# The opening loads of a fused attention and feed-forward kernel: weights in two pieces, the first pair in halves, V by pairs, and one later load

## The chip, the cores and the metric

The kernel runs on one core of one Trainium2 chip. The metric is the device time of one execution in microseconds (us), as a median over several executions. A core has five engines that run their own instruction streams and wait for each other through semaphores: TensorE (PE, matrix products), VectorE (DVE), ScalarE (ACT, activation functions), GpSimd (POOL) and SyncE (SP, which here only issues DMAs). [...]

## The reference

The reference computes cosine attention and then a feed-forward layer with the activation h * cos(h). B = 8 batches, H = 12 heads, S = 448 positions, D = 64; the model width is 768, the hidden width 2048.

```python
q_n = q / (norm(q) + 1e-6);  k_n = k / (norm(k) + 1e-6)      # over D
scores = q_n @ k_n.T / tau
attn = softmax(scores)
x = (attn @ v) as [B*S, H*D]                                  # 3584 x 768
h = x @ w_in                                                  # 768 x 2048
out = (h * cos(h)) @ w_out                                    # 2048 x 768
```

## The kernel before

**Units and pairs.** The 12 heads of a batch are two units of six heads, so there are 16 units, u0 to u15. A unit is three pairs of heads; the 48 pairs are numbered g = 0 to 47, and pair g works on two heads at once. Six pairs make one batch. In the text below "the third pair of unit 3" is g = 11, the twelfth pair of all.

**Normalisation of a pair.** `load` (L596) fetches k into partitions 0 to 63 and q into partitions 64 to 127 of a float32 buffer `raw`; there are two such buffers, so unit u + 2 can be loaded for a pair only after unit u has been scaled for it. Each partition holds seven blocks of 64 numbers for each head. `square` (L629) squares into `sq`, on ACT for the first pairs and on POOL later. `reduce` (L643) sums on DVE. `rnorm` (L654) makes the reciprocal root, with two activations on ACT (L667, L670: logarithm and exponential) or with an addition and a power on POOL (L663, L664), by the list `roots`. `scale` (L673) multiplies into the bfloat16 buffer `qks`, on POOL; for the very first pair POOL takes the first four blocks (half a) and DVE the last three (half b). `transposes` (L691) turns the pair: for g below 9 PE transposes into PSUM (bank TP, a part of the tile MP) and DVE copies to `qkT` (L716); from g = 9 on a DMA transpose that SP issues does it (L695).

**Attention of a pair.** `scores` (L719) makes four score tiles on PE (L735 a half one, L727 three full ones), and ACT takes their exponentials into `PX` (L742). `attend` (L801) multiplies with V on PE (L821, L828, and the row sums at L845 and L858); ACT makes the reciprocal of the sums (L887 and L889, or L901 and L903) and DVE or POOL writes the normalised, transposed x into `xT` (L893, L907, L940).

**Feed-forward.** `m1` (L960) is the first product, x @ w_in, for one batch: 16 blocks of 128 hidden columns in eight steps of two, each of six accumulated matmuls (L953). The n-th block needs the weight quarter n // 4. After each step ACT takes the cosine (L982) and DVE the product (L984) into `gT`; the key ("gT", 0, y) stands for step y of batch 0. The second product (L1052 and L1081) is cut into small pieces, which fill PE's time between the scores of the later pairs. Its weights W2 come in four quarters, its result leaves through `osb` (L1019, L1016) and SP.

**Loads.** All q and k loads are issued by SP, in a fixed order. V (`load_v`, L609) and the weights (`load_w1`, L1098, and `load_w2`, L1104) are issued by POOL. V of one unit is two DMAs of 192 KB; W1 comes in four quarters of 768 KB, W2 in four. The first pair's k and q are two loads on SP (`apart`), each with its own semaphore; V of unit 0 waits until the first q has landed, V of unit 1 and the first two quarters of W1 until half a of the first pair has been scaled (key ("qks", 0, 0, 0)).

**Order.** A planner (`Program.arrange`, L152) plays the program with costs for each instruction and DMA, and each engine's stream is then emitted in the order of that play. So a change of a load, a gate or a cost can move instructions on every engine. PE additionally gets filler matmuls (L1111) where the play leaves it idle before the first product. The order of the rest, the six pairs of batch 0, then the first product of batch 0, then pairs 6 to 47 with the second product between them, and a first product after every sixth pair or so, is written out at the end of the program (L1242 to L1324).

## Time and profile before

| | |
|---|---|
| median of 3 executions | 416.63 us (415.61 to 416.63) |
| profiled execution | 415.4 us, span 413.6 us |
| granted PE clock | 1.00 in every stretch |
| PE busy | 404.6 us (98%) |
| POOL busy | 248.5 us (60%) |
| ACT busy | 270.2 us (65%) |
| bytes moved by DMA | 63.99 MB, mean 155 GB/s |

The profile is of one execution. The time of that execution is 1.8 us more than its span, which runs from the first to the last instruction. "Busy" is the sum of an engine's instructions. PE's sum counts pipelined matmuls, so it says that PE had something to do, not that it ran at its peak. In rows of instructions in order of time the first number is the start in us from the span's start, the second the time taken, and in brackets stands how long the engine idled before it and what released it. In rows of DMA issues the last number is the time from issue to landing.

### The profile page before, as it was taken

What the parts mean: (1) busy time and instruction counts of PE and PEld (TensorE: products, weight loads), DVE (VectorE), ACT (ScalarE), POOL (GpSimd) and SP (SyncE); (2) the same over time, 40 slices, a digit from 0 to 9 for tenths busy, and PEclk for the clock granted to TensorE, in tenths of its full rate; (3) what the DMA queues carried; (4) which work ended last, traced back from release to release, by engine and by line L of the source; (5) the groups of instructions that cost most, each with busy time, mean ns of one, the idle gap of its engine ahead of it and who ended that gap; (6) DMA issues with size and microseconds to landing.
All of it is one profiled execution on the core that took longest, in us unless ns stands there. A gap on an engine that the chain in (4) does not pass through costs nothing.

```text
span 413.6 us, 13910 instructions
## 1 busy us (share of the span) xinstructions
PE 404.6 (98%) x6213; PEld 243.8 (59%) x6213; DVE 199.9 (48%) x279; ACT 270.2 (65%) x384; POOL 248.5 (60%) x196
## 2 busy tenths in 40 slices
PE   7899999999999999999999999999999999999997
PEld 3354556655566655765567656865567655655555
DVE  4574653426664457445644567344742344413421
ACT  5897578985889745985497647884488745623500
POOL 4999995894776985988489656946482303020000
PEclk9999999999999999999999999999999999999999
DMA  8999999489997999586988975797933531151023
GB/s 183 248 252 226 207 222 202 136 157 215 178 163 164 228 258 188 121 205 149 206 101 188 268 132 113 135 215 188 169 51 79 147 85 32 46 139 38 2 73 81
DMA packets 78736, 63.99 MB, mean 155 GB/s; under 512 B 41844, under 2 KB 72404, under 8 KB 78676
## 3 DMA queue, kind: packets, MB, share of 16 engines
q1 hardware_dynamic: 60468, 50.42, 54.4%
q0 software_dynamic: 18048, 12.59, 20.7%
q8 instruction: 49, 0.80, 0.8%
q10 hardware_dynamic: 160, 0.10, 0.1%
q14 instruction: 11, 0.09, 0.1%
HBM read 55.44 MB, written 11.19 MB: 161 GB/s over the span
## 4 chain that ended last, share of the span: by engine, by line
PE 91%; POOL 3%; ACT 2%; DVE 2%; DMA 1%; issue 0%; SPq 0%; ACTq 0%; POOLq 0%
PE MP L1052 27%; PE SC L953 20%; PE AV L953 12%; PE SC L727 7%; PE AV L764 5%; PE MP L1081 4%; PE AV L788 4%; PE SC L1081 3%; PE MP L953 2%; PE AV L837 2%; POOL qks L678 1%; PE SC L735 1%; ACT cosb L982 1%; PE MP L852 1%; PE AV L1081 1%; DMA raw<-in_q_dram 1%
## 5 line engine op out<-in xcount | busy, mean ns | idle before, releaser
L742 ACT ACTIVATE PX<-SC 128x448 bf16<-128x448 f32 (+1 forms) x192 | 148.7, 825 | 16.0 <-PE SC L727 10.9
L1052 PE MATMUL MP<-W,gT 64*64 64x384 bf16 x2816 | 136.2, 323 | 0.7 <-DVE qkT L716 0.6
L1052 PEld LDWEIGHTS MP<-W,gT 64*64 64x64 bf16 x2816 | 80.1, 107 | 34.5 <-issue 3.9
L953 PE MATMUL SC<-xT,W 128*128 128x448 bf16 x444 | 90.9, 353 | 0.0
L678 POOL TENSOR_TENSOR qks<-raw,rn 128x896 bf16<-128x896 f32 (+1 forms) x48 | 79.8, 1679 | 12.0 <-ACT rn L670 11.6
L640 POOL TENSOR_TENSOR sq<-raw 128x896 bf16<-128x896 f32 x44 | 73.9, 1686 | 11.8 <-DMA raw<-in_q_dram 6.4
L940 POOL TENSOR_TENSOR xT<-xu,RB 128x448 bf16<-128x448 f32 x36 | 40.1, 1135 | 67.7 <-DMA RB<-scr 67.7
L953 PEld LDWEIGHTS SC<-xT,W 128*128 128x128 bf16 x444 | 43.1, 98 | 40.2 <-ACT osb L1016 0.4
L982 ACT ACTIVATE cosb<-SC,cst 128x896 f32<-128x896 f32 x37 | 37.2, 1006 | 37.8 <-PE SC L953 35.9
L953 PE MATMUL AV<-xT,W 128*128 128x448 bf16 x276 | 59.6, 352 | 0.0
L647 DVE TENSOR_REDUCE n<-sq 128x14 f32<-128x896 bf16 (+2 forms) x49 | 51.6, 1059 | 7.1 <-ACT sq L638 4.8
L984 DVE TENSOR_TENSOR gT<-SC,cosb 128x896 bf16<-128x896 f32 x37 | 40.3, 1090 | 28.2 <-ACT cosb L982 28.1
L727 PE MATMUL SC<-qkT 64*64 64x448 bf16 x576 | 51.9, 354 | 0.3
L982 ACT ACTIVATE cosb<-AV,cst 128x896 f32<-128x896 f32 x23 | 23.1, 1006 | 37.1 <-PE AV L953 35.4
L774 DVE COPY xu<-AV 128x448 f32<-128x448 f32 x36 | 22.5, 624 | 50.4 <-PE AV L756 50.4
L953 PEld LDWEIGHTS AV<-xT,W 128*128 128x128 bf16 x276 | 26.6, 98 | 25.4 <-DVE xs L799 1.1
L764 PE MATMUL AV<-PX,va 64*64 64x448 bf16 x432 | 38.2, 349 | 0.0
L614 POOL DMA_DIRECT2D va<-in_v_dram x32 | 22.0, 694 | 22.9 <-DVE gT L984 18.2
L1019 DVE COPY osb<-MP 128x384 f32<-128x384 f32 x26 | 14.5, 558 | 43.9 <-PE MP L1052 32.8
L984 DVE TENSOR_TENSOR gT<-AV,cosb 128x896 bf16<-128x896 f32 x23 | 25.0, 1087 | 20.3 <-ACT cosb L982 20.3
L727 PEld LDWEIGHTS SC<-qkT 64*64 64x64 bf16 x576 | 16.7, 106 | 13.0 <-ACT PX L742 6.3
L775 DVE TENSOR_TENSOR xu<-xu,AV 128x448 f32<-128x448 f32 x36 | 22.4, 621 | 1.2
(84 smaller groups left out, 364.7 us busy)
## 6 DMA issues: line engine op xcount, KB each, us to landing
raw<-in_k_dram SPq DMA_DIRECT2D x48, 224.0 KB, 5.4
raw<-in_q_dram SPq DMA_DIRECT2D x48, 224.0 KB, 5.9
out_dram<-osb SPq DMA_DIRECT2D x54, 192.0 KB, 3.1
RB<-scr SPq DMA_DIRECT2D x22, 336.0 KB, 5.2
va<-in_v_dram POOLq DMA_DIRECT2D x32, 192.0 KB, 6.1
W<-in_moe_w_in_dram POOLq DMA_DIRECT2D x4, 768.0 KB, 15.0
W<-in_moe_w_out_dram POOLq DMA_DIRECT2D x4, 768.0 KB, 20.0
qkT<-qks SPq DMA_TRANSPOSE x39, 4.4
```

The lines of the kernel that those rows point to most:

```text
L640: pool(lambda e, x=x, y=y: e.tensor_tensor(y, x, x, ALU.mult), src_, dst, 0.1 + n * 1.78e-3, label="sq%d.%d" % (u, p)).pad = LATE if u > 1 ...
L647: dve(lambda e, w=w: e.tensor_reduce(out=n2v[i][:, 2 * p : 2 * p + 2, w], in_=sqv[p][:, :, w, :], axis=mybir.AxisListType.X, op=ALU.add), ...
L678: f = lambda e, s0=s0, s1=s1: e.tensor_tensor(qksv[i][:, p, s0:s1].rearrange("p s h d -> p h s d"), rawv[i][:, h, s0:s1, :], bass.AP(rn[i] ...
L727: m = e.matmul(SCv[z][BP * o : BP * o + BP, a, 0:S], t[r, c - 1 + (NT3 + 1) * o, 0:BP], t[r, :, BP : 2 * BP], start=True, stop=True)
L742: act(lambda e: e.activation(PHv[j] if c == 0 else PXv[j][:, c - 1], SCv[z][:, :, 0:n], ACT.Exp, scale=1.0 / TAU), ["SC%d" % z], [("PX", j ...
L764: m = e.matmul(AVv[64 * a : 64 * a + 64, o, 0:S], vav[y][r, 2 * p + a, c + 1, :], PXv[j][r, c, a, :], start=(c == 0), stop=False)
L940: f = lambda e, p=p: e.tensor_tensor(xTv[b % 2][:, UP * i + p, :].rearrange("p (s o m) -> p o s m", s=NB, o=2), xuv[:, u % 3, p, :].rearra ...
L953: t = e.matmul(ph[:, a, 0:S], W1v[:, order[c], 128 * n : 128 * n + 128], xTv[b % 2][:, order[c], :], start=(c == 0), stop=(c == NKC - 1))
L982: act(lambda e, ph=ph, cz=cz: e.activation(cosv[cz], ph[:, :, 0:S], ACT.Sin, bias=cst.ap()[:, 0:1], scale=1.0), names(gi) + ["cst0"], [("c ...
L984: dve(lambda e, ph=ph, cz=cz, gi=gi: e.tensor_tensor(gTv[:, 2 * gi : 2 * gi + 2, S * (b % 2) : S * (b % 2) + S], ph[:, :, 0:S], cosv[cz], ...
L1052: r = e.matmul(POH[b][x : x + 64, 0:HW], gTv[k, y, col + x : col + x + 64], W2v[k, y, HW * b : HW * b + HW], start=(y == 0 and h == 0), st ...
L1081: r = e.matmul(po[:, 0 : w[1] - w[0]], gTv[:, y, col : col + 128], W2v[:, y, w[0] : w[1]], start=(y == 0), stop=(y == NF - 1))
```

## The change

1. *Weights.* `load_w1` takes the cuts from a list, `w1`: two loads of 1024 columns (1.5 MB each) instead of four of 512. The first product's blocks 0 to 7 wait for the first, blocks 8 to 15 for the second. POOL issues the first after the scale of the fourth pair (the first of unit 1), the second after the scale of the fifth; before, the first quarter was issued ahead of the second pair's scale.
2. *First pair.* k and q of the first pair come in halves, four blocks and three; SP issues k's halves and ACT q's halves. ACT does so before it loads its activation table. The square of each half waits only for its own half, and is followed by that half's norm; ACT's squares of the second and third pair come after both.
3. *V.* V of unit 0 comes as two DMAs for its first pair, issued when k's first half has landed, and two for the other two pairs, issued after half a of the first pair is scaled, ahead of V of unit 1.
4. *Unit 3's third pair.* Its k and q load waits for step 5 of the first product of batch 0 (its sixth block pair), its square, sum and scale follow later on POOL and DVE, and its norm goes to ACT. Unit 4's first load waits for step 7 instead of step 6.
5. *Planner.* Some of its constants and rules are changed (issue times, how two queues share, when POOL's first DMAs start), which moves instructions. On PE the fillers are 32 instead of 38; in the first six pairs the first matmuls of a pair's product with V (L821) stand before the next pair's scores instead of behind them in some places; from pair 6 to 8 the pieces of the second product stand in other places between the scores. On DVE the second pair's reduction stands behind the first pair's half b scale and first copy, the third pair's behind its second copy; one reduction (unit 3's third pair) no longer stands before the third copy at the end of the first product. From the second first product on (batch 1) PE's order is the same.

```diff
-    "u4": (6,),
+    "u4": (7,),
...
+    "gates": "xcccac",
+    "openers": ("SP", "ACT"),
+    "v0": ((0, 1), (1, 3)),
+    "together": 1,
+    "w1": (0, 2, 4),
+    "split3": {2: 5},
...
-    "roots": (3, (8, 0), (10, 0), (12, 0), (14, 0)),
+    "roots": ((3, 0), (3, 1), (8, 0), (10, 0), (12, 0), (14, 0)),
...
-    TAKEOFF = {"SP": 1.85, "ACT": 1.85, "POOL": 1.6}
+    TAKEOFF = {"SP": 1.85, "ACT": 1.85, "POOL": 1.9}
...
+        if apart:
+            for z in range(2):
+                s0, s1 = blocks((z,))
+                for x, t in enumerate((k, q)):
+                    go = lambda e, x=x, t=t, s0=s0, s1=s1: e.dma_start(
+                        rawv[i][BP * x : BP * x + BP, h, s0:s1, :].rearrange("p h s d -> p h (s d)"),
+                        bass.AP(t.tensor, ((u // 2) * NH + UH * (u % 2) + 2 * p0) * S * D + s0 * D, [[NB * D, BP], [S * D, 2], [1, (s1 - s0) * D]]))
+                    dma(PLAN["openers"][x], [go], list(reads), [("part", x, z)] + (["first"] if x == 0 and z == 0 else []), "part%d_%d" % (x, z),
...
+        if u == 0:
+            for (p0, p1), reads in zip(PLAN["v0"], reads):
+                dma("POOL", [lambda e, z=z, p0=p0, p1=p1: e.dma_start(
...
+                    list(reads), [("vp", p) for p in range(p0, p1)], "vp%d" % p0, 0.707 * (p1 - p0), "load v u0", None)
+            return
...
     def load_w1(x, behind=None, reads=()):
-        w = FF // NQ
+        c0, c1 = [FF // NQ * y for y in PLAN["w1"][x : x + 2]]
         dma("POOL", [lambda e: e.dma_start(
-            W1v[:, :, w * x : w * x + w], bass.AP(moe_w_in.tensor, w * x, [[FF, 128], [128 * FF, NKC], [1, w]]))],
...
+            W1v[:, :, c0:c1], bass.AP(moe_w_in.tensor, c0, [[FF, 128], [128 * FF, NKC], [1, c1 - c0]]))],
...
-    loads(3)
+    for x in range(UP):
+        if x not in PLAN["split3"]:
+            load(3, x, x + 1)
     norms(3, 0)
...
+    for x, y in PLAN["split3"].items():
+        load(3, x, x + 1, reads=[("gT", 0, y)])
+        square(3, x, "P")
+        reduce(3, x)
     norms(3, 1)
```

## The prediction

> **What bounds the kernel now.** I read the page's first two parts, then busy time by stretch, then each engine's instructions in order of time up to the first product, then the DMA issues.

> ```profile
> span 413.6 us, 13910 instructions
> PE 404.6 (98%) x6213; PEld 243.8 (59%) x6213; DVE 199.9 (48%) x279; ACT 270.2 (65%) x384; POOL 248.5 (60%) x196
> ```
> ```profile
> 10.00:20.00 10.00, 8.03 (x105) 3.72 (x104) 5.49 (x8) 8.49 (x18) 10.00 (x8) 1.00 1.22 247
> 20.00:30.00 10.00, 9.82 (x161) 5.73 (x163) 6.81 (x10) 9.46 (x19) 9.96 (x8) 1.00 1.18 253
> 30.00:40.00 10.00, 9.99 (x114) 4.61 (x113) 4.89 (x8) 8.76 (x15) 9.97 (x10) 1.00 1.22 229
> 50.00:60.00 10.00, 9.21 (x128) 5.65 (x130) 5.77 (x7) 6.66 (x8) 9.75 (x9) 1.00 1.16 219
> 300.00:350.00 50.00, 49.99 (x881) 30.90 (x883) 20.39 (x27) 34.05 (x46) 18.24 (x14) 1.00 0.36 81
> ```
> Columns: stretch, its length, busy PE, PEld, DVE, ACT, POOL, then granted clock, DMA share, GB/s. PE has no room in the late stretches (49.99 of 50), and the changed kernel gives it the same work there. So only the head can move: from 10 to 40 POOL is full, ACT nearly, and the DMA engines are saturated, while PE has small work and fillers; from 50 to 60 PE loses 0.79 us. What the head gains, the end gains, unless a later stall eats it.

> ```profile
> 5.44 1.04 ACT L638 ACTIVATE sq<-raw 128x512 bf16<-128x512 f32 x2 [3.44 <-DMA raw<-in_q_dram]
> 9.25 0.95 ACT L638 ACTIVATE sq<-raw 128x896 bf16<-128x896 f32 x1 [0.55 <-DMA raw<-in_q_dram]
> 11.35 0.31 ACT L667 ACTIVATE rn<-n,cst 128x14 f32<-128x14 f32 x1 [0.71 <-DVE n L647]
> 11.98 1.35 ACT L742 ACTIVATE PX<-SC 128x448 bf16<-128x448 f32 x2
> 13.77 2.16 ACT L742 ACTIVATE PX<-SC 128x896 bf16<-128x896 f32 x3 [0.43 <-PE SC L727]
> 34.70 1.70 ACT L742 ACTIVATE PX<-SC 128x896 bf16<-128x896 f32 x2
> ```
> ```profile
> 7.52 1.04 POOL L678 TENSOR_TENSOR qks<-raw,rn 128x512 bf16<-128x512 f32 x1 [0.34 <-ACT rn L670]
> 8.86 1.35 POOL L614 DMA_DIRECT2D va<-in_v_dram  x2 [0.30 <-POOL qks L678]
> 10.17 0.89 POOL L1100 DMA_DIRECT2D W<-in_moe_w_in_dram  x1
> 11.05 1.73 POOL L678 TENSOR_TENSOR qks<-raw,rn 128x896 bf16<-128x896 f32 x1
> 20.89 0.90 POOL L1100 DMA_DIRECT2D W<-in_moe_w_in_dram  x1
> 25.98 1.70 POOL L678 TENSOR_TENSOR qks<-raw,rn 128x896 bf16<-128x896 f32 x1
> ```
> Each row is start, duration, instruction. ACT idles 3.44 us for the first q, 0.71 and 0.43 us more around the first exponentials, and has no gap over 0.21 us from there to the last pair's. POOL's last scale of the six pairs ends at 27.7, but that pair's exponentials run only up to 36.4: from the second pair on the head is ACT's, and POOL runs ahead of it.

> **The change part by part.**

> *First pair in halves on two queues.*
> ```profile
> raw<-in_k_dram SPq DMA_DIRECT2D x1, 224.0 KB, 3.6
> raw<-in_q_dram SPq DMA_DIRECT2D x1, 224.0 KB, 3.8
> ```
> k is issued at 0.72 and lands at 4.3; q, issued at 1.54, lands at 5.35, so 224 KB take about 1.0 us. The first halves hold 4 of 7 blocks, 256 KB of 448: q's last 192 KB (0.86 us) need not be waited for. Landing 4.5; bounds 3.9 (k's half and q's half moving side by side at k's rate) and 5.35 (no gain). The second halves still land near 5.35. ACT now issues two loads (0.6 to 0.76 us each) ahead of its table load (1.28 us): done by 3.5, hidden before 4.5.

> The norm of half a then ends some 0.8 us earlier: ACT takes half b's square first, at 5.35, so 5.9 instead of 6.5. The scale of half a starts at 6.7, not 7.52.

> *The order on DVE and ACT.*
> ```profile
> 8.30 1.09 DVE L647 TENSOR_REDUCE n<-sq 128x14 f32<-128x896 bf16 x1 [1.05 <-ACT sq L638]
> 10.23 1.09 DVE L647 TENSOR_REDUCE n<-sq 128x14 f32<-128x896 bf16 x1
> 11.24 0.35 DVE L716 COPY qkT<-AV 128x384 bf16<-128x384 bf16 x1
> 11.64 0.29 PE L735 MATMUL SC<-qkT 64*64 64x224 bf16 x4 [0.26 <-DVE qkT L716]
> ```
> Before, two reductions for later pairs stand ahead of the first pair's second copy; after, one does. Scale a 6.7 to 7.75, transposes to 8.2, copy to 8.65, reduction to 9.7, copy to 10.05: first scores at 10.1, not 11.64. But ACT now squares the third pair (its q lands at 9.25, ends 10.2) before the second pair's norm, so exponentials start at 10.7. The first pair's four then end at 10.7 + 3 x 0.87 + 0.45 + 0.5 (the third pair's norm between them) = 14.3; before, at 13.77 + 2 x 0.87 = 15.5. Lead 1.2 us; I take 1.1, as the second pair's scores come only just in time (scale 10.7 to 12.4, transposes 13.1, copy 13.8).

> *POOL.* V of unit 0 is four issues instead of two (1.35/2 = 0.68 each, +1.35), W1 two instead of four (-1.8). After scale a at 7.75 stand four V issues, 8.0 to 10.7; W1's issue at 10.17 is gone. The second pair's scale starts at 10.7, not 11.05: POOL gains only 0.35 us. Up to the last scale (25.98) it has the same work, so that ends at 27.35, against exponentials due at about 31: hidden. The split V hides too: its first pair, issued at 4.4, is wanted at 13, and DMAs of 192 KB issued at 5.65 landed from 12.6.

> *W1 in two.* The first product needs its first load.
> ```profile
> 34.06 1.69 PE L953 MATMUL MP<-xT,W 128*128 128x448 bf16 x8
> W<-in_moe_w_in_dram POOLq DMA_DIRECT2D x1, 768.0 KB, 20.9
> W<-in_moe_w_in_dram POOLq DMA_DIRECT2D x1, 768.0 KB, 15.2
> va<-in_v_dram POOLq DMA_DIRECT2D x1, 192.0 KB, 14.5
> q0 software_dynamic: 890, 0.90, 75.8%
> q1 hardware_dynamic: 548, 0.87, 41.2%
> ```
> (The last two rows: packets and MB of POOL's and SP's queue from 24 to 31.) Before, quarter one lands at 31.1, quarter two at 20.89 + 15.2 = 36.1. Now both are one load, issued near 18.9. As V of unit 1 keeps POOL's queue busy until 9.5 + 14.5 = 24.0, nothing is lost by the later issue: the queue carries the same bytes, and would finish at 36.1. Out of the way are unit 3's third q and k, 0.46 MB at 250 GB/s: 34.2, the late bound. The rows give the other: 890 packets of POOL's queue went beside 548 of SP's, and the new packets hold twice the bytes; with this ratio kept POOL's queue moves 1.25 MB in those 7 us instead of 0.90, and 1.57 MB take 8.8 us, from 23.7 to 32.5, the early bound. PE comes to it at 34.06 - 1.1 = 32.95. I take 32.5, since only the packet rows show both queues at once: no stall. At 34.2 it would cost 1.2 us, all of the lead.

> [...]

> *Unit 3's third q and k behind block six; its norm from POOL to ACT.*
> ```profile
> 27.71 0.59 SPq L599 DMA_DIRECT2D raw<-in_k_dram  x1
> 55.09 1.08 DVE L647 TENSOR_REDUCE n<-sq 128x14 f32<-128x896 bf16 x1
> 56.08 0.61 DVE L716 COPY qkT<-MP 128x896 bf16<-128x896 bf16 x1
> 56.84 1.50 PE L1052 MATMUL MP<-W,gT 64*64 64x384 bf16 x32 [0.64 <-DVE qkT L716]
> 57.20 2.62 POOL L664 TENSOR_TENSOR rn<-rn,cst 128x14 f32<-128x14 f32 x1
> 68.35 1.25 SPq L695 DMA_TRANSPOSE qkT<-qks  x1
> 78.44 0.27 PE L735 MATMUL SC<-qkT 64*64 64x224 bf16 x4
> ```
> The reduction at 55.09 leaves its place before the copy that the second product waits for: copy at 55.8, 0.25 us won. The two issues (27.71, 1.6 us) move to about 51; behind them SP has only unit 4's first load, itself put one block later, and a transpose at 59.5 held by PE. Landing 59, square, unit 4's square (its load lands about 65), scale to 68, transpose at 68.4 as before, landed by 73, wanted at 78.44: 5 us of cover. POOL loses 2.9 us of power; ACT gets 0.5 us of norm near 63, beside a full PE: nothing, at most 0.5.

> *Second product's first tile.* Its pieces stand earlier between the scores after 57, so W2's last quarter is wanted near 61.5 instead of 63.5.
> ```profile
> 42.00 0.80 POOL L1106 DMA_DIRECT2D W<-in_moe_w_out_dram  x1
> W<-in_moe_w_out_dram POOLq DMA_DIRECT2D x1, 768.0 KB, 20.5
> ```
> It landed at 62.5; 1.85 us come off it for the moved q and k, and go on again when these land at 59: between 60.6 and 62.5, so nothing to 1 us. I take nothing, since POOL now issues all of W2 some 5 us earlier. Six of PE's 38 fillers go; they stood in idle time.

> *Sum.* -1.1 (head) -0.25 (copy) = -1.35 us. The profiled execution took 415.4 (span 413.6): 414.05. It ran 1.2 under the median of 416.63; put against the median it gives 415.3. I forecast 415.2.

> **Rivals.**
> 1. *The weights take the head's place.* W1's first load lands at 34.2 by bytes alone, PE waits for it, and only the copy's 0.25 to 0.6 remain: 416.2. For it: the DMA share of 1.2 all through the head. Against: the packet rows.
> 2. *Slower: a descriptor costs the same whatever its size.* Then the four half loads take 4.0 us instead of 2.0, the third pair lands at 11.2, the exponentials start at 12.7, 0.7 later than now, and W1 is 2 us later too: the first product starts between 34.75 and 36.2 (W1's late bound), which less the copy's 0.25 gives 417.1 to 418.5, 417.8 in the middle. It decides once the third pair lands after 10.5. Against: a queue at 1.8 KB and one at 1 KB packets share the engines at 250 GB/s, so time goes with bytes.
> 3. *More than forecast.* The halves move side by side (3.9), unit 2's loads no longer share with W1, and PE's other waits from 56 to 64 close: 0.8 more, 414.4 or under.

> [...]

> **How the numbers follow.** Forecast 45%, rival 1 25%, rival 3 15%, rival 2 10%, and 5% for W1 after 35. A measurement tells about 0.3%, 1.25 us, from no change, so 415.4 is the edge to faster: four fifths of the forecast and all of rival 3 lie beyond it, 0.52; the rest of the forecast and rival 1 make 0.33; 0.15 slower. Range 413.3 (rival 3 from the profiled time) to 417.3, short of rival 2; the forecast's own 414.1 to 416.

> **What would show it.** Right: ACT's first square near 4.5, exponentials from 10.7, the first L953-type product at 33.0 with no wait on a W load, the second product's first row near 55.5. Wrong: an idle row of PE released by W's DMA before the first product, the third pair's square after 10, or a wait on qkT at the twelfth pair's scores.

## The result, and the profile after

| | median of 22 | lowest and highest | profiled execution |
|---|---|---|---|
| kernel before | 416.07 us | 415.32 to 417.34 | 415.4 us, span 413.6 |
| changed kernel | 417.96 us | 415.28 to 420.59 | 416.0 us, span 414.2 |

The changed kernel takes 1.0047 of the time of the kernel before (95% interval 1.0032 to 1.0063): it is slower by 1.9 us, where 1.35 us less had been forecast, and 417.96 lies above the forecast's range (413.3 to 417.3). The second thing to see is the scatter: 5.3 us between the lowest and the highest run, against 2.0 before. The profiled execution is a lucky one, near the lowest of all. Two more profiles were therefore taken, of executions of 415.4 and 419.58 us; the last is slower than 18 of the 22 runs and shows what a slow one loses. In two of the kernels below, one run lay over 1.5% above the fastest of its kernel (422.18 and 421.99 us) and is left out of their ratios.

The changed kernel's page, and its busy time by stretch (columns as in the prediction):

```profile
span 414.2 us, 13901 instructions
PE 405.2 (98%) x6207; PEld 243.6 (59%) x6207; DVE 200.3 (48%) x279; ACT 269.5 (65%) x386; POOL 245.0 (59%) x194
```
```profile
30.00:40.00 10.00, 7.80 (x95) 3.38 (x95) 3.62 (x6) 6.64 (x12) 9.98 (x10) 1.00 1.12 220
50.00:60.00 10.00, 9.44 (x116) 5.59 (x118) 6.32 (x8) 6.06 (x7) 6.33 (x6) 1.00 1.19 226
60.00:70.00 10.00, 10.00 (x252) 6.57 (x247) 4.80 (x7) 8.99 (x15) 3.36 (x2) 1.00 1.14 202
200.00:250.00 50.00, 49.48 (x828) 30.34 (x826) 26.55 (x35) 32.96 (x45) 36.22 (x28) 1.00 0.86 170
```
From 50 to 70 PE gained 0.5 us (9.21 and 9.72 before). From 30 to 40 it lost 2.2, and 0.4 from 200 to 250. The head in order of time, ACT first, then POOL, then PE:

```profile
4.14 0.63 ACT L670 ACTIVATE sq<-raw 128x512 bf16<-128x512 f32 x1 [0.69 <-DMA raw<-in_k_dram]
5.67 0.52 ACT L670 ACTIVATE sq<-raw 128x384 bf16<-128x384 f32 x1 [0.90 <-DMA raw<-in_k_dram]
9.65 0.95 ACT L670 ACTIVATE sq<-raw 128x896 bf16<-128x896 f32 x1 [1.07 <-DMA raw<-in_q_dram]
10.51 0.29 ACT L701 ACTIVATE rn<-n,cst 128x14 f32<-128x14 f32 x1
10.95 1.33 ACT L777 ACTIVATE PX<-SC 128x896 bf16<-128x896 f32 x2
33.18 1.71 ACT L777 ACTIVATE PX<-SC 128x896 bf16<-128x896 f32 x2
```
```profile
6.78 1.04 POOL L712 TENSOR_TENSOR qks<-raw,rn 128x512 bf16<-128x512 f32 x1 [0.94 <-ACT rn L704]
11.19 1.69 POOL L712 TENSOR_TENSOR qks<-raw,rn 128x896 bf16<-128x896 f32 x1 [0.45 <-ACT rn L704]
19.39 0.89 POOL L1135 DMA_DIRECT2D W<-in_moe_w_in_dram  x1
```
```profile
10.13 0.29 PE L770 MATMUL SC<-qkT 64*64 64x224 bf16 x4 [0.35 <-DVE qkT L751]
34.81 1.69 PE L988 MATMUL MP<-xT,W 128*128 128x448 bf16 x8 [2.20 <-DMA W<-in_moe_w_in_dram]
```
The last pair's exponentials stand at 33.18 instead of 34.70: the head has its gain, 1.5 us. Then PE waits 2.20 us for W1's first load, and the first product starts at 34.81 instead of 34.06. And the second scale, which the forecast had at 10.7, stands at 11.19 and waits for ACT: there the second pair's roots (10.51) stand behind the third pair's square, and that waited 1.07 us for its load.

The execution of 419.58 us, what PE waited for after the first product's place, and the rows:

```profile
PE AV L988 <- DVE gT L1019: 1.7, 1, 1.7
PE MP L988 <- DMA W<-in_moe_w_in_dram: 1.5, 1, 1.5
PE MP L1087 <- issue: 0.7, 1, 0.7
PE MP L1087 <- DVE qkT L751: 0.4, 1, 0.4
```
```profile
19.20 0.28 PE L856 MATMUL AV<-PX,va 64*64 64x224 bf16 x1 [0.78 <-DMA va<-in_v_dram]
35.22 1.69 PE L988 MATMUL MP<-xT,W 128*128 128x448 bf16 x8 [1.49 <-DMA W<-in_moe_w_in_dram]
73.80 0.67 PE L1087 MATMUL MP<-W,gT 64*64 64x384 bf16 x10 [0.71 <-issue]
293.51 2.43 PE L988 MATMUL AV<-xT,W 128*128 128x448 bf16 x12 [1.75 <-DVE gT L1019]
```
Four stops of different kinds: V of unit 0's second and third pair late (issued at 8.20, its second DMA landed at 19.15), W1 late, 0.71 us of "issue" (PE waits for no engine and no load that the profile shows), and at 293.51 a product that waits for DVE behind a chain of q and k loads which SP issued late (one at 285.04 that stands at 280.65 in the execution of 416.0 us). The kernel before has none of them.

W1's landing can be read from the DMA rows. From 24 to 31 us, the window of the prediction's two packet rows, POOL's queue moved this in the execution of 416.0 us:

```profile
q0 software_dynamic: 524, 1.07, 80.9%
q1 hardware_dynamic: 385, 0.63, 28.7%
```
That is 1.07 MB where the forecast's early bound had 1.25, and 1.4 packets to one of SP's instead of 1.6. V of unit 1, which stands ahead of W1 in this queue, landed at 24.56 us; 1.57 MB more at 1.07 MB in 7 us take 10.3 us, which gives 34.8, and W1 landed at 34.76.

So it pays to cut every profile in two: the start of the first product, and the rest of the span.

| profiled execution | first product starts | rest of the span |
|---|---|---|
| kernel before | 34.06 | 379.5 |
| changed, 416.0 us | 34.81 | 379.4 |
| changed, 415.4 us | 33.57 | 380.0 |
| changed, 419.58 us | 35.22 | 382.6 |

### The profile page after: what moved, and what is told of

The parts are those of the page before. It is cut to its first block, busy times and chain, and to the rows that moved or that the text cites. A ratio compares the mean times of both kernels' runs of the same rounds, so it can differ in the third digit from the quotient of the medians.

```text
span 414.2 us, 13901 instructions
## 1 busy us (share of the span) xinstructions
PE 405.2 (98%) x6207; PEld 243.6 (59%) x6207; DVE 200.3 (48%) x279; ACT 269.5 (65%) x386; POOL 245.0 (59%) x194
## 3 DMA queue, kind: packets, MB, share of 16 engines
HBM read 55.44 MB, written 11.19 MB: 161 GB/s over the span
## 4 chain that ended last, share of the span: by engine, by line
PE 88%; DMA 5%; POOL 2%; ACT 2%; DVE 1%; SPq 1%; issue 0%; ACTq 0%; POOLq 0%
PE MP L1087 27%; PE SC L988 20%; PE AV L988 12%; PE SC L762 6%; PE AV L799 5%; PE MP L1116 4%; PE AV L823 4%; DMA W<-in_moe_w_in_dram 4%; PE SC L1116 3%; PE MP L988 2%; PE AV L872 2%; DMA raw<-in_q_dram 1%; POOL qks L712 1%; PE SC L770 1%; ACT cosb L1017 1%; PE AV L1116 1%
## 5 line engine op out<-in xcount | busy, mean ns | idle before, releaser
L777 ACT ACTIVATE PX<-SC 128x448 bf16<-128x448 f32 (+1 forms) x192 | 148.8, 825 | 15.9 <-PE SC L762 10.3
L1087 PEld LDWEIGHTS MP<-W,gT 64*64 64x64 bf16 x2816 | 80.2, 107 | 33.8 <-issue 3.7
L674 POOL TENSOR_TENSOR sq<-raw 128x896 bf16<-128x896 f32 x44 | 73.8, 1687 | 16.1 <-DMA raw<-in_q_dram 10.9
L1017 ACT ACTIVATE cosb<-SC,cst 128x896 f32<-128x896 f32 x37 | 37.2, 1006 | 38.1 <-PE SC L988 36.2
L1054 DVE COPY osb<-MP 128x384 f32<-128x384 f32 x26 | 14.5, 558 | 43.1 <-PE MP L1087 31.9
L645 POOL DMA_DIRECT2D va<-in_v_dram x30 | 20.6, 691 | 18.1 <-DVE gT L1019 18.1
## 6 DMA issues: line engine op xcount, KB each, us to landing
raw<-in_k_dram SPq DMA_DIRECT2D x47, 224.0 KB, 4.8
raw<-in_q_dram SPq DMA_DIRECT2D x47, 224.0 KB, 5.1
out_dram<-osb SPq DMA_DIRECT2D x54, 192.0 KB, 3.4
va<-in_v_dram POOLq DMA_DIRECT2D x30, 192.0 KB, 6.8
W<-in_moe_w_out_dram POOLq DMA_DIRECT2D x4, 768.0 KB, 19.7
```

The source lines that it names most:

```text
L674: pool(lambda e, x=x, y=y: e.tensor_tensor(y, x, x, ALU.mult), src_, dst, 0.1 + n * 1.78e-3, label="sq%d.%d" % (u, p)).pad = LATE if u > 1 ...
L777: act(lambda e: e.activation(PHv[j] if c == 0 else PXv[j][:, c - 1], SCv[z][:, :, 0:n], ACT.Exp, scale=1.0 / TAU), ["SC%d" % z], [("PX", j ...
L1017: act(lambda e, ph=ph, cz=cz: e.activation(cosv[cz], ph[:, :, 0:S], ACT.Sin, bias=cst.ap()[:, 0:1], scale=1.0), names(gi) + ["cst0"], [("c ...
L1087: r = e.matmul(POH[b][x : x + 64, 0:HW], gTv[k, y, col + x : col + x + 64], W2v[k, y, HW * b : HW * b + HW], start=(y == 0 and h == 0), st ...
```

## The experiments

"Order held" means that the planner's order on every engine was kept and only the named instructions were exchanged, split or joined; otherwise the planner made a new order. A ratio below is not the quotient of the two medians given with it, so the two can differ a little. Five theories came up in turn: A, W1's first load is late and all the loss is there; B, the moved third load; C, the halves and V hold up the third pair; D, TensorE's own instructions come late; E, no part, but the newly planned order that goes with them.

### Second and third profile of the changed kernel

> The changed kernel once more, unaltered, for a second profiled execution. Theory A (the weights): W1's first 1.5 MB load lands after TensorE wants it; it landed at 34.8 us in the profile of a 416.0 us execution, and the scatter of the runs (415.3 to 420.6) is the scatter of this landing. So in an execution of about 418 us TensorE stands some 4 us ahead of the first product (2.2 in the one seen), the load lands at 36 to 37 us, and what follows the first product is as before to 0.3 us. Theory B (the moved third q and k load of unit 3 and the second product's new order): the stop ahead of the first product is again about 2.2 us, and a slower execution has its loss behind 50 us.

> The changed kernel again, for a third profiled execution; the first two had only 416.0 and 415.4 us, among runs of which half are over 417.9. Theory A (W1's first load lands late): if this one is slow, TensorE's stop ahead of the first product is 3 us or more (2.2 and 1.5 in the two seen). Theory C (the third pair's landing): ScalarE's square of the third pair starts at 10.2 us or later (9.65 and 9.14 in the two seen), GpSimd's second scale at 11.8 us or later, and the last exponentials start over 33.8 us. Theory D (TensorE's own instructions come late): gaps on TensorE behind 50 us that no engine and no load ends, 1 us and more together.

Measured: 417.88 us (415.4 to 420.3, 12 runs), ratio 1.0052 (1.0032 to 1.0073); profiled at 415.4 and, in the other run, at 419.58. The slow one has a stop for W1 of only 1.49 us, ACT's third square at 9.80 and the second scale at 11.34: neither A nor C explains the 4 us between the two. Part of it (0.71) is D, and 1.75 us is a fourth cause.

### W1 in quarters, or in three loads, in the changed kernel

```diff
-W1.0: quarters 0, 1 | W1.1: quarters 2, 3              # changed kernel
+q0, q1 in the place of W1.0 | q2, q3 in that of W1.1   # quarters
+q0 in the place of W1.0 | q1 in that of W1.1 | q2+q3 ahead of W2's first   # three loads
```

> The changed kernel with every engine's order held, but each of W1's two loads issued as two loads of 768 KB, one right behind the other, and the first product's steps waiting for their own quarter. Theory A: the first quarter lands at 30 to 32 us, TensorE's stop ahead of the first product falls from 2.2 us to under 0.5, the median to 413.6 to 415.0 us, and the runs lie as close together as those of the kernel before (within some 2 us). Theory B: no gain, 417 us or more.

> The changed kernel with its order held, W1 in three loads: the first quarter where the first load was, the second quarter where the second load was, the other half behind GpSimd's next square, so that GpSimd issues no more loads ahead of its last scale than in the changed kernel. Theory A: the first quarter lands at 30 to 31.5 us, TensorE's stop ahead of the first product falls below 0.5 us, median 415.0 to 416.0 us (1.9 to 2.9 below the changed kernel). Theory C: at most 0.5 us of that, 417.4 us or more. Theory D: no gain, 417.5 us or more, with gaps behind 50 us.

Measured: quarters 418.38 us, ratio 1.0058 (1.0037 to 1.0080); three loads 420.11, ratio 1.0080 (1.0056 to 1.0105). Both took the stop for W1 away, and neither won anything. PE of the kernel with three loads, and the TensorE clock (the number after the five busy times) around its second gap:

```profile
33.26 1.69 PE L988 MATMUL MP<-xT,W 128*128 128x448 bf16 x8
67.39 0.35 PE L872 MATMUL AV<-PX,va 64*64 64x448 bf16 x1 [1.30 <-issue]
75.14 0.92 PE L1087 MATMUL MP<-W,gT 64*64 64x384 bf16 x10 [2.09 <-issue]
```
```profile
74.00:76.00 2.00, 0.86 (x16) 0.73 (x19) 0.00 (x0) 0.00 (x0) 1.53 (x1) 0.86 1.31 181
76.00:78.00 2.00, 2.00 (x32) 1.57 (x27) 0.00 (x0) 1.02 (x2) 0.43 (x1) 0.50 0.26 49
```
The first product starts at 33.26, 0.8 us ahead of the kernel before: A was right on what W1 costs ahead of the product. But 1.30 and 2.09 us of "issue" follow, and the clock falls to a half for some 3 us. So A alone does not explain the loss. What are these gaps? Two queues are named "instruction" in the DMA view; q8 carries 49 packets of 0.80 MB in all, some 16 KB each, and 12,426 of some 13,900 instructions are TensorE's matmuls and weight loads, so these are read here as its code; the section on gaps and code packets bears this out. In the changed kernel's 415.4 us execution and in that with three loads, the stretch from 60 to 62 us:

```profile
DMA packets 724, 0.50 MB, mean 249 GB/s; under 512 B 449, under 2 KB 723, under 8 KB 723
...
q8 instruction: 1, 0.02, 8.1%
```
```profile
DMA packets 605, 0.53 MB, mean 265 GB/s; under 512 B 35, under 2 KB 605, under 8 KB 605
...
q0 software_dynamic: 414, 0.22, 77.8%
q1 hardware_dynamic: 191, 0.31, 49.2%
```
and in the latter from 64 to 66 us:

```profile
DMA packets 479, 0.23 MB, mean 114 GB/s; under 512 B 399, under 2 KB 478, under 8 KB 478
...
q8 instruction: 1, 0.02, 4.6%
```
The packet comes at 60.9 us in the one (without a gap) and at 64.5 in the other (gap until 67.39); the packet ahead of it comes at 52.8 and 52.6. The table of all profiles below carries this through.

### Joining W1 in the kernel before

```diff
-W1.0 at 10.2, W1.1 at 20.9, W1.2 at 25.1, W1.3 at 30.9 us
+W1.0+W1.1 at 10.0, W1.2+W1.3 at 24.5 us
```

> The kernel before with every engine's order held, but W1 in two loads of 1.5 MB, issued where the first and the third quarter were. Theory A: the first load lands at 33 to 37 us, and TensorE, which came to the first product at 34.06 us, waits up to 3 us for it: median 416.5 to 419, runs as scattered as those of the changed kernel (over 4 us). Theory B: within 0.4 us of the kernel before.

Measured: 415.62 us against 415.47, ratio 0.9998 (0.9988 to 1.0008), no scatter. The load lands at 34.2 us, and PE, 0.26 us of wait included, starts at 34.19. Two loads cost nothing where the head has no lead to lose.

### The third load put back in the changed kernel

```diff
-"split3": {2: 5}, "u4": (7,), "roots": ((3, 0), (3, 1), ...
+"split3": {},     "u4": (6,), "roots": (3, ...
```

> The changed kernel with the last part undone: unit 3's third q and k load, its squares and its reduction back where the kernel before has them, and its two settings (unit 4's loads, the roots of unit 3) put back; the two loads of W1, the halves and V by pairs stay. Theory A: 417 to 419 us and as scattered as the changed kernel, with the same stop ahead of the first product. Theory B: 416 us or less.

> The changed kernel with the third load put back (as in the run that measured 419.5 us) and with that run's order held, W1 as a quarter, a quarter and a half. Theory D and theory A together: no stop ahead of the first product, none behind it, so the first product at 33.3 to 34.0 us and 379.7 us behind it: 414.8 to 415.6 us and little scatter. Theory D wrong: 417 us or more, with the same gaps at 66 to 76 us as with the third load moved.

Measured: 419.53 us, ratio 1.0092 (1.0058 to 1.0126); with three loads of W1, 421.53, ratio 1.0133 (1.0103 to 1.0163). B finds no support: without the moved load the kernel, planned anew, is slower. W1's first load then lands at 36.8, and the stop is 3.55 us long. PE and its clock:

```profile
36.81 3.17 PE L988 MATMUL MP<-xT,W 128*128 128x448 bf16 x8 [3.55 <-DMA W<-in_moe_w_in_dram]
```
```profile
36.00:38.00 2.00, 1.19 (x4) 0.52 (x5) 0.00 (x0) 0.22 (x1) 2.00 (x3) 0.71 1.14 225
38.00:40.00 2.00, 2.00 (x10) 0.60 (x8) 0.00 (x0) 0.00 (x0) 2.00 (x2) 0.50 1.12 213
```
Eight matmuls take 3.17 us instead of 1.69: by the clock rows and that of 40 to 45 (0.97) the stop costs some 1.7 us more afterwards (0.29 x 2, 0.50 x 2 and 0.03 x 5, an estimate). With three loads there are gaps of 1.3 and 2.0 us again, so the moved load does not make them, though D had supposed that it did.

### The coupling on ACT

```diff
 ACT:  square 0.1
-      square 0.2; roots 0.1
+      roots 0.1; square 0.2
```

> The changed kernel with one exchange on ScalarE: the second pair's two root steps ahead of the third pair's square, so that GpSimd's second scale no longer waits for the third pair's landing; all else in its order. Theory A: within 0.4 us of the changed kernel (417.5 to 418.3), since an earlier end of the head only lengthens the stop for W1. Theory C: GpSimd's second scale starts at 10.7 to 10.9 us whatever the third pair does, median 0.5 to 1.5 us below the changed kernel, and the runs closer together (within 3 us). Theory D: as the changed kernel.

> Both edits: the second pair's roots ahead of the third pair's square, and W1 as a quarter, a quarter and a half. Theory A: as with W1 in three loads alone, 415.0 to 416.0 us. Theory C with A: 414.3 to 415.3 us, which would be below the kernel before. Theory D: 417 us or more.

Measured: 416.99 us, ratio 1.0025 (1.0007 to 1.0042); with three loads of W1 besides, 419.99, ratio 1.0104 (1.0061 to 1.0147). The exchange moves the second scale as C says, and its median is some 0.9 us lower than the changed kernel's, though the runs still lie 3.9 us apart and the interval overlaps the changed kernel's (from 1.0032). POOL's row:

```profile
10.63 1.76 POOL L712 TENSOR_TENSOR qks<-raw,rn 128x896 bf16<-128x896 f32 x1
```

### The halves on the kernel before, with V early and V late

```diff
-SP: k, q (224 KB each)
+SP: k 128 KB, k 96 KB | ACT: q 128 KB, q 96 KB; squares, scales wait for their half
 V of unit 0, whole, waits for
-  q
+  k's first half (V early)   or   q's second half (V late)
```

> The kernel before with its order held and one part of the change: the first pair's q and k as half loads, k on SP, q on ScalarE's queue, and V of unit 0 issued once the first half of k is in (as one load, not by pairs). W1 stays in quarters, unit 3's third load where it was. Theory A (all the loss lies in W1's two loads) and theory D (TensorE's instructions come late behind data, which the moved third load and the new order of the second product bring about) agree here: the second scale on GpSimd at 10.3 instead of 11.05 us, the first product at 33.3 to 33.8 instead of 34.06 us, what follows it as long as in the kernel before (379.5 us of span), median 0.3 to 1.0 us below it, runs as close together as its own. Theory C (the halves and V hold up the third pair): no gain or a loss, the third pair's square at 9.8 us or later.

> The kernel before with its order held and the halves alone; V of unit 0 waits for the whole first pair, as in the kernel before. If V's earlier start (4.45 instead of 5.65 us) is what delays the third pair: third pair's square at 9.2 to 9.5 us (10.06 with V early), second scale at 10.7 to 11.1 us, median within 0.3 us of the kernel before. If the halves themselves delay it: square at 9.8 us or later, median 0.6 to 1.2 us above the kernel before, as with V early.

Measured: V early 416.84 us against 415.74, ratio 1.0024 (1.0010 to 1.0038); V late 415.83 against 416.05, ratio 0.9999 (0.9987 to 1.0011). ACT and POOL with V early, then with V late:

```profile
10.06 0.95 ACT L638 ACTIVATE sq<-raw 128x896 bf16<-128x896 f32 x1 [1.01 <-DMA raw<-in_q_dram]
```
```profile
11.61 1.68 POOL L678 TENSOR_TENSOR qks<-raw,rn 128x896 bf16<-128x896 f32 x1 [1.48 <-ACT rn L670]
```
```profile
9.47 0.95 ACT L638 ACTIVATE sq<-raw 128x896 bf16<-128x896 f32 x1 [0.55 <-DMA raw<-in_q_dram]
```
```profile
11.01 1.68 POOL L678 TENSOR_TENSOR qks<-raw,rn 128x896 bf16<-128x896 f32 x1 [0.58 <-ACT rn L670]
```
With V late the halves cost nothing. With V early, issued at 4.45 instead of 5.33 us in the same us as the third pair's loads, these land 0.6 us later and the kernel is 1.0 us slower. The 0.6 us are a difference of one profile each, and the three profiles of the changed kernel spread over as much (9.12 to 9.78 us), so only the time is clear. This V is the whole 384 KB of unit 0; the changed kernel issues 128 KB that early, and V by pairs was not run alone. The rest of the span is 379.5 us with V early, as before.

### The moved load alone, with two loads, with three

```diff
 kernel before
+load(3, 2, 3, reads=[("gT", 0, 5)]); square; reduce; roots of unit 3 on ACT; "u4": (7,)
+  and W1 as two loads (second kernel), or as q0 | q1 | q2+q3 (third kernel)
```

> The kernel before with only the other part: unit 3's third q and k load behind the first product's sixth block with its square, reduction and ScalarE roots, unit 4's loads one block later, planned anew. The head is that of the kernel before. Theory D: the second product's order becomes that of the changed kernel, what follows the first product lasts 1 to 3 us longer in half of the runs, with gaps of TensorE that no engine or load ends between 60 and 76 us or a late load near 290 us: median 416.5 to 418.5 us, scatter 3 us or more. Theory A: within 0.3 us of the kernel before, or up to 0.4 faster by the reduction that is gone, and no scatter.

> The kernel before with two of the three parts, W1 in two loads (issued where the first and third quarter were) and the moved third load; no halves, no V by pairs. If the loss is in one of these two parts or in their sum: 416.8 us or more. If it needs the halves or the order that goes with them (theories C and E): 415.2 to 416.0 us.

> The kernel before with the moved third load, and W1 as a quarter, a quarter and a half, the first two issued where they were, the half where the last quarter was, so that GpSimd issues one load fewer ahead of its last scale. The last scale starts at 25.1 to 25.4 instead of 25.98 us, the first product at 33.3 to 33.8 instead of 34.06 us with its quarter long in, 379.0 us behind it: 414.3 to 415.3 us, below both kernels. If TensorE's instructions come late once it is earlier (gaps at 60 to 76 us): 415.7 us or more.

Measured: alone 415.63 against 415.74 us, ratio 1.0001 (0.9986 to 1.0016), but from 414.44 to 417.61; with two loads 416.01, ratio 0.9999 (0.9984 to 1.0013); with three 418.28, ratio 1.0060 (1.0041 to 1.0079). The second product's new order alone is no loss: its profiled rest is 378.8, 0.7 under the kernel before. The version with three loads was expected to beat both kernels and lost 2.2 us: its last scale came only 0.3 us earlier (25.70), the first product 0.1 (33.98), and gaps of 0.95 and 1.35 us followed at 67 and 74. The same parts with W1 in two loads or in four have no such gap.

### The halves undone in the changed kernel

```diff
-k and q of the first pair in halves on SP and ACT
+k and q whole on SP; all else, V by pairs too, in the changed kernel's order
```

> The changed kernel with its order held and the halves alone undone: the first pair's k and q as one load each, both on SP; V of unit 0 by pairs, W1's two loads and the moved third load stay. Theory C (in the changed kernel the loss comes by the halves and their second queue): 416 us or less, scatter under 3 us. Theory E (the loss comes from the order that was planned around the halves: W1's first load issued at 19.4 instead of 10.2 us, V earlier, the second scale behind the third pair's square): 417.2 us or more and a scatter of 4 us, since all of that stays.

Measured: 418.12 us (417.82 without the run left out), ratio 1.0052 (1.0028 to 1.0076), 415.54 to 420.93 in the eleven runs that count. As slow and as scattered as with the halves: the halves are not what costs, so that half of C falls for the changed kernel, and E stands. V by pairs stays in this kernel, so V is not ruled out.

### All parts but V by pairs in the old order; W1 issued early in the new order

```diff
 first: kernel before
+halves (V late), W1 in two loads at 9.5 and 24.3 us, third load moved
 second: changed kernel, POOL
-V u1; scale 0.1; square; scale 0.2; square; scale 1.0; W1.0
+V u1; W1.0; scale 0.1; square; scale 0.2; square; scale 1.0
 third: the second
+and ACT's roots 0.1 ahead of square 0.2
```

> The kernel before with all parts of the change but V by pairs, in the order of the kernel before: the first pair by halves on two queues (V of unit 0 waiting for the whole pair, as before), W1 in two loads issued where the first and the third quarter were, the third load moved. If the parts themselves cost nothing (theory E: the loss comes by the new plan, that is V earlier, W1's first load at 19.4 instead of 10 us and the second scale behind the third pair's square): 415.3 to 416.4 us. If the parts lose together: 417 us or more.

> The changed kernel with one exchange on GpSimd: W1's first load issued right behind V of unit 1 (at about 10.7 us, as in the kernel before) instead of behind the scale at 17.8 us; all else in its order. If the late issue is what makes that load late (33.5 to 37 us in the changed kernel): it lands at 33 to 34.2 us, the stop ahead of the first product is under 1 us, median 0.7 to 2 us below the changed kernel (416.0 to 417.3). If the issue time does not matter, since the queue is full with V until 23 us anyway: within 0.5 us of the changed kernel, 417.4 to 418.5 us.

> The same with the second pair's roots ahead of the third pair's square as well (which alone took 0.9 us off the median). If both the late issue and the coupling to the third pair cost time: 415.2 to 416.3 us, as fast as the kernel before or faster. If only the coupling does: 416.8 to 417.5 us.

Measured against 415.57 us: all parts but V by pairs 415.17, ratio 0.9985 (0.9971 to 0.9998), the only kernel here whose interval lies below the kernel before, though by 0.15% alone; W1 early 416.80, ratio 1.0025 (1.0009 to 1.0042); W1 early and the roots first 416.58 (416.48 without the run left out), ratio 1.0010 (0.9993 to 1.0027). That last interval does not meet that of the changed kernel (from 1.0032): the two exchanges together take away most of the loss; each alone halves it by the medians, with intervals that overlap the changed kernel's a little. By what way they help is not shown: with both, POOL's second scale stands at 11.26 us, no earlier than in the changed kernel, since W1's issue now stands ahead of it. W1 early stopped PE for 1.72 us in its profiled execution, and with the roots first not at all:

```profile
34.51 1.69 PE L988 MATMUL MP<-xT,W 128*128 128x448 bf16 x8 [1.72 <-DMA W<-in_moe_w_in_dram]
```
```profile
32.77 1.69 PE L988 MATMUL MP<-xT,W 128*128 128x448 bf16 x8
```
The kernel with all parts but V by pairs, on POOL and PE:

```profile
10.76 1.68 POOL L678 TENSOR_TENSOR qks<-raw,rn 128x896 bf16<-128x896 f32 x1 [0.36 <-ACT rn L670]
```
```profile
33.72 1.50 PE L953 MATMUL MP<-xT,W 128*128 128x448 bf16 x7
```
It is 0.34 us earlier at the first product and has the old rest (379.5). It differs from the changed kernel in two ways at once, the order of the head and V by pairs, so it shows that the other parts cost nothing in this order and does not tell those two apart.

For the issue time, here is the landing of W1's first load of 1.5 MB in all profiles that have it, with that of V of unit 1, which stands ahead of it in POOL's queue:

| profiled kernels | W1 issued at | V of unit 1 landed at | W1 landed at | behind V |
|---|---|---|---|---|
| changed (three), halves undone, roots first, third load back | 19.4, 18.9, 19.5, 19.5, 18.8, 20.0 | 24.6, 22.9, 25.6, 23.9, 25.0, 23.3 | 34.8, 33.5, 35.2, 34.0, 34.6, 36.8 | 10.2, 10.7, 9.5, 10.2, 9.6, 13.4 |
| W1 joined, W1 early, W1 early and roots first, all but V by pairs, third load with two loads | 10.0, 10.3, 10.4, 9.5, 9.9 | 23.4, 25.1, 22.3, 22.6, 22.0 | 34.2, 34.5, 32.7, 33.3, 33.0 | 10.8, 9.3, 10.5, 10.7, 11.0 |

The mean landing is 34.8 against 33.5 us. But V of unit 1 lands 1.1 us earlier in the second group too, and three of its five kernels have no V by pairs and the old order. Counted from that landing W1 takes 9.3 to 11.0 us in ten of the eleven, issued late or early. So these profiles do not show that the issue time counts; W1's landing follows that of the load ahead of it. The early issue moved POOL's own time as well: the scales of the fifth and sixth pair and POOL's loads up to 34 us come 0.9 us earlier than in the changed kernel's first profile.

### Gaps and code packets in all profiles

Distance is that between the code packet near 53 us (57.7 with the third load back) and the next, read in steps of 0.5 us; gaps are PE's "issue" waits from 60 to 80 us.

| profiled kernels | distance | gaps |
|---|---|---|
| before; W1 joined; third load alone; with two loads; halves, V early; halves, V late; changed at 416.0 and 415.4; roots first; third load back; W1 early | 7.5 to 10.0 | none |
| all but V by pairs | 10.5 | none |
| changed at 419.58; halves undone; third load with three; W1 early, roots first | 10.5 | 0.7, 1.0, 2.3 and 1.5 |
| changed with quarters, with three loads, with three and roots first; third load back with three | 11.0 to 12.0 | 2.3, 3.4, 2.1 and 3.3 |

With a limit between 10.0 and 10.5 us nineteen of these twenty profiles fall as D says; the exception is the second row. Read to the hundredth, that row is at 10.07 and the third at 10.16 to 10.44, so the split is a narrow one. It speaks of one packet alone, too, while eight of the thirteen larger stops, those from 72 to 75 us, come one packet later.

The places of the stops say more. Here are the two stops of the kernel with the third load moved and W1 in three loads, and the stretch between them, from the one restart to the other:

```profile
66.96 0.37 PE L837 MATMUL AV<-PX,va 64*64 64x448 bf16 x1 [0.95 <-issue]
73.89 0.84 PE L1052 MATMUL MP<-W,gT 64*64 64x384 bf16 x16 [1.35 <-issue]
66.96:73.89 6.93, 5.58 (x127) 3.76 (x128) 2.24 (x3) 5.12 (x10) 4.03 (x3) 1.00 1.12 236
```
These are 127 matmuls, the weight loads that go with them and two recorded instructions of PE's control: 256 in all. Past 30 us the twenty profiles have 22 "issue" waits of PE over 0.25 us, and all of them stand ahead of the 727th, 854th, 1614th or 3771st matmul (give or take one), in the old order and in the new. Counted in PE's recorded instructions, the second place is 256 behind the first, the third 6 x 256 and the fourth 23 x 256 behind the second; and 49 packets for some 12,550 recorded instructions make 256 to a packet. Each of the 22 waits ends 1.3 to 1.7 us behind the end of a code packet. In no profile does PE pass a place of this spacing sooner than 1.2 us behind its packet. Read from these times, PE stands there because its next instructions have not come: D holds for these 22 waits.

PE needs 5.3 us for 256 instructions here when nothing stops it (66.48 to 71.81 us in the kernel before). The packets for the 727th and the 854th matmul start soon after PE has passed the place 256 instructions earlier: up to 3.3 us behind it where PE then stops for under 0.25 us or not at all, and 3.4 to 4.9 us behind it in the 13 larger stops. Why they start late is not shown. Ahead of the first of the two, POOL's queue (W2's last quarter and V of unit 3) and many small packets, read here as the transposes', are on the engines. Ahead of the second, POOL's queue moves nothing, and SP's alone fills the engines, as from 67.4 to 72.3 us with W1 in three loads:

```profile
q1 hardware_dynamic: 1606, 1.11, 113.0%
```
No run took this traffic away. The changed kernel's 0.4 us from 200 to 250 is such a stop too: at the 3771st matmul, near 235 us, eight of the twelve profiles with the changed kernel's order of the head wait 0.4 to 1.3 us, and none of the other eight does.

## Why the prediction was wrong, point by point

**First halves, norm and first scores: right.** Squares at 4.14 and 5.67 us (forecast 4.5 and 5.35), half a's scale at 6.78 (6.7), first scores at 10.13 (10.1), first exponentials at 10.95 (10.7). The lead at the last exponentials was 1.5 us in the first profile and 0.4 in the third.

**"From the second pair on the head is ACT's, and POOL runs ahead of it": failed.** The forecast saw that ACT squares the third pair ahead of the second pair's roots, and charged it to the exponentials alone. POOL's second scale hangs on the same roots. The forecast had it at 10.7; it came at 11.19, 10.68 and 11.34, following the third pair's load, which landed at 9.63, 9.12 and 9.78. The exchange on ACT took about 0.9 us off the median, with intervals that overlap. "The split V hides too" is not borne out either: PE waited for V of unit 0's later pairs in the third profile (0.78 us at 19.20), with the roots first (0.50) and with the halves undone (0.23), and a whole V started early cost 1.0 us. What V by pairs costs by itself was not run.

**W1 landing at 32.5, "no stall": failed, and this is the step with the largest error.** Of the bounds 32.5 and 34.2 the early one was taken, from a ratio of packets. Measured: 34.8, 33.5 and 35.2, so two of three even behind the late bound. That the ratio stays when POOL's packets double was an estimate that no run shows: it went from 1.6 to 1.4 in the first profile, and POOL's queue moved 1.07, 1.04 and 1.07 MB from 24 to 31 us, not 1.25. The lead of the head came (PE stood ready at 32.6, 32.1 and 33.7 instead of 34.06), but the sum put the stop for W1 at nothing, and PE then stood 2.20, 1.48 and 1.49 us. With that the first product starts 0.47 us later than before in the mean of the three, not 1.1 us earlier. The premise "nothing is lost by the later issue" is not refuted: W1 lands some 10 us behind V of unit 1 whether it is issued early or late. Rival 1 had this mechanism at 34.2, close to the mean of 34.5, but its 416.2 was short by 1.8 us: it gave the load one landing time where the changed kernel's three profiles alone differ by 1.7 us, and it left the rest of the span as it was.

**What the rest of the span does: not forecast, the second step that failed.** The sum took the rest as 0.25 us shorter and otherwise fixed. The copy's 0.25 came as forecast (PE's wait there is 0.40 instead of 0.64 us), and the stretches from 50 to 70 won 0.5. But the rest is 379.4, 380.0 and 382.6 us against 379.5: 0.4 and 0.6 us of late code near 234 in the first two, and 0.71 of late code and 1.75 at 293.51 in the third. And where W1's stop was taken from the changed kernel, by quarters or three loads, stops for code took its place. No rival had either; a PE at 49.99 of 50 was read as proof that nothing there could move, where it only said that nothing did.

**Rival 2** gave 417.8, nearly the measured time, by a mechanism that did not happen: the third pair lands at 9.63 us, ahead of its deciding point of 10.5, and the halves alone cost nothing. That its time is the nearest is luck. Rival 3's side-by-side halves came near: q's landed at 3.61 and k's at 4.12, against 3.9 there and 4.5 in the forecast; in the kernel before the whole loads, both on SP's queue, landed 1.0 us apart (4.37 and 5.35).

**W2's last quarter and the twelfth pair** were rightly taken as nothing: no wait on either in the changed kernel's profiles.

**Sums and readings.** With the ratio of 890 to 548 kept and POOL's packets twice as large, the same 1.77 MB hold 1.2 MB of POOL's queue, not 1.25; that moves the early bound from 32.5 to 32.9, still ahead of PE's 32.95. Four fifths of 45% and 15% make 0.51, not 0.52.

**What stays open.** The changed kernel loses 0.47 to 0.52%. W1 issued early and the roots ahead of the third square together bring this to 0.10% (-0.07 to 0.27), but not by an earlier issue as such, and their way is not shown. V by pairs and the other moves of the new order were not told apart. Why the chain of late q and k loads reaches PE near 290 us in some executions (1.75, 1.6, 0.9, 0.5 us, or not at all; the 0.9 us stand in a kernel with the old head), and what delays the code packets, was not tried.

TensorE's clock after a stop is open too: it was 0.50 behind the stop of 3.55 us (38 to 40 us, third load back) and behind one of 2.09 us (76 to 78 us, three loads), and 1.00 behind the changed kernel's 2.20 us. What decides between them was not shown.

## What to carry to other kernels

A load that PE must have is priced by the range of its landings, not by one value, and from the landing of the load ahead of it in its queue (here 9.3 to 11.0 us behind it in ten of eleven profiles): if several things end within a us of each other, each adds its late cases to the time and none adds its early ones. When an instruction is moved ahead of another in an engine's stream, follow every engine that waits for either, not only the one on which the forecast's bound lies. And before judging the parts of a change that a planner has spread over the whole order, put the parts into the old order: here all of them but V by pairs were 0.15% faster there, and the whole change was 0.47% slower in the new one.
